# Cosine attention and an MLP mixer on one core: two-tile scores, ScalarE norms, a permuted w2, and the last residual by DMA transposes and VectorE adds

## The chip, the cores and the metric

The kernel runs on one core of one Trainium2 chip. The metric is device microseconds of one execution, measured over several executions. TensorE does the matmuls, VectorE and GpSimd elementwise work, ScalarE activations; SP issues most transfers, GpSimd those that cast.

In the profile's lines PE is TensorE, PEld its weight loads, DVE is VectorE, ACT is ScalarE, POOL is GpSimd, and SPq is SP issuing transfers. A matmul's recorded duration contains pipeline latency (a residual matmul is recorded with 219 ns, while the next one starts 56 ns later), so I measure a matmul's cost from one start to the next.

## The reference, cut to what matters

```python
q_n = q / (norm(q) + 1e-6);  k_n = k / (norm(k) + 1e-6)         # (8, 12, 448, 64)
attn = softmax(q_n @ k_n.T / tau)
x = (attn @ v) as (8, 448, 768)
h = relu(x.T @ w_tok1) @ w_tok2            # mixing over the 448 tokens
u = x + h.T
out = u + relu(u @ w_ch1) @ w_ch2          # (8, 448, 768), float32
```

## The kernel before

The unit of work is a pair of heads; there are 48 pairs, six per batch. Iteration i of the main loop computes the scores of pair i, attn @ v of pair i-1, and the token mixing of an earlier pair; once a batch's six pairs are done, its channel mixing (12 units `m_ch1`, then 6 or 8 output units `m_ch2`) is fed in between. For q and k the squares are made on GpSimd, summed on VectorE, and turned into 1/(norm + eps) by ScalarE and VectorE.

```python
ps = ctx.enter_context(tc.tile_pool(name="ps", bufs=4, space=PSUM))
ps2 = ctx.enter_context(tc.tile_pool(name="ps2", bufs=1, space=PSUM))
# ... cut ...
    def sums(i):
        lo = 2 * NCH * (i % HP)
        nc.vector.tensor_reduce(out=half[i // HP]["ssq"][:, :, lo:lo + 2 * NCH], in_=pipe[i]["sq"][:],
                                axis=AXX.X, op=ALU.add)

    def rnorms(n, p0=0, p1=HP):
        # ... cut ...
        nc.scalar.activation(out=rn, in_=ssq, func=AF.Ln, bias=tiny[:])
        nc.scalar.activation(out=rn, in_=rn, func=AF.Exp, scale=0.5)
        nc.vector.tensor_scalar_add(out=rn, in0=rn, scalar1=EPS_NORM)
        nc.vector.reciprocal(out=rn, in_=rn)

    def score(i, cg):
        # ... cut ...
        psS = ps2.tile([128, 2, 2, 512], FP32, name=f"psS_{i}_{cg}", tag="s")       # four banks, one buffer
        # four matmuls of 448 columns
        nc.scalar.activation(out=st["pt"][:, cg], in_=psS[0:SC, :, :, 0:S], func=AF.Exp, scale=inv_tau)

    def m_tok2(i):
        # ... cut ...
        for tt in range(TT):
            nc.tensor.matmul(psU[:], st["r"][:, tt, :], w2t[:, tt, 0:S], start=(tt == 0), stop=False)
        for c in range(NCH):                    # adds x; writes every fourth column of psU
            nc.tensor.matmul(psU[:].rearrange("d (p c) -> d c p", c=NCH)[:, c, :], st["x"][:, c, :],
                             id16[:, LEAD[c]:LEAD[c] + SC], start=False, stop=(c == NCH - 1))
        # VectorE copies psU to ut (u transposed, fp16)

    def m_ch2(b, m, dh):
        # ... cut ...
        for ct in range(CT):
            nc.tensor.matmul(psF[:], rows(gt, ct), wc2t[:, ct, dh * DH:(dh + 1) * DH],
                             start=(ct == 0), stop=False)
        for i in range(3):                      # the residual: u comes back through an identity
            nc.tensor.matmul(psF[:, 128 * i:128 * (i + 1)], rows(ut, 3 * dh + i), id16[:],
                             start=False, stop=(i == 2))
        if dh == 0:
            nc.vector.tensor_copy(out=o[:, 0:DH], in_=psF[:])
        else:
            nc.scalar.copy(out=o[:, DH:D], in_=psF[:])
    # ... cut ...
    # main loop, end of iteration i
            for p in sq_at.get(i, ()):
                sums(p)
                if p < 15:
                    rnorm1(p)                   # ScalarE: stands ahead of the exps of pair i+1
```

## Time and profile before

| | before |
|---|---|
| time, median of the first 3 runs | 456.56 us (456.43 to 456.67) |
| span of the profiled run | 455.0 us |
| TensorE busy, whole span / first 100 us | 408.4 us / 59.8 us |
| first score of iteration 8 / 10 / 13 | 66.6 / 95.0 / 118.1 us |
| from iteration 13 to the end | 336.9 us |

The last two rows are read from the timeline of TensorE: the start of the first score matmul of the iteration.

The page of the kernel before: busy tenths in 40 slices of the span, and the granted TensorE clock in tenths.

```profile
PE   1377572899999999999999999999999999999995
...
PEclk9999987899999999999999999999999999999998
```

There are two regimes. From the ninth slice on TensorE is at 9 all the way; before, it is not, and in the seventh slice the clock falls too. The table of busy time by stretch puts numbers on it (columns: stretch, its length, busy us of each engine with its instruction count, granted clock, mean busy share of the 16 DMA engines, which is over 1 where packets overlap in time, and GB/s):

```profile
20.00:40.00 20.00, 15.12 (x168) 10.04 (x168) 11.39 (x27) 12.44 (x13) 16.77 (x18) 1.00 1.14 243
40.00:60.00 20.00, 13.48 (x194) 9.98 (x191) 12.69 (x30) 11.22 (x12) 14.52 (x15) 0.92 0.84 174
60.00:80.00 20.00, 9.46 (x120) 6.04 (x117) 15.25 (x23) 7.20 (x11) 16.69 (x17) 0.84 0.75 147
...
120.00:160.00 40.00, 39.47 (x406) 23.90 (x404) 16.41 (x38) 23.08 (x27) 20.20 (x20) 1.00 0.51 132
```

Between 60 and 80 us no engine is full. That is the sign of a chain that runs from engine to engine. ScalarE's timeline of the kernel before shows its shape (start, duration, engine, line, operation, then idle time before it and what ended it):

```profile
62.10 0.31 ACT L162 ACTIVATE rn_382<-ssq_381,tiny 112x16 f32<-112x16 f32 x1 [2.58 <-DVE ssq_381 L155]
62.44 0.22 ACT L163 ACTIVATE rn_382<-rn_382 112x16 f32<-112x16 f32 x1
62.56 1.65 ACT L210 ACTIVATE pt_827<-psS_0_828 112x1792 f16<-112x1792 f32 x1
```

The exp at 62.56 us had its scores in PSUM since about 61 us, but stood behind the norms of a later pair (L162), and these waited 2.6 us for VectorE's sum. TensorE in turn waits for the exp. VectorE's timeline of the kernel before, around the largest loss:

```profile
69.20 0.17 DVE L164 TENSOR_SCALAR rn_382<-rn_382 112x16 f32<-112x16 f32 x1 [0.62 <-ACT rn_382 L163]
...
71.36 6.27 DVE L164 TENSOR_SCALAR rn_382<-rn_382 112x16 f32<-112x16 f32 x1 [0.62 <-ACT rn_382 L163]
```

The same add takes 0.17 us once and 6.27 us the next time. GpSimd's timeline over the second one has no gap:

```profile
71.57 1.05 POOL L176 TENSOR_TENSOR qn_924<-qh_378,rn_382 112x512 f16<-112x512 f32 x1
72.58 1.04 POOL L176 TENSOR_TENSOR kn_926<-kh_379,rn_382 112x512 f16<-112x512 f32 x1
73.58 1.03 POOL L150 TENSOR_TENSOR sq_928<-qh_701 112x512 f32<-112x512 f32 x1
...
76.57 1.03 POOL L150 TENSOR_TENSOR sq_931<-kh_702 112x512 f32<-112x512 f32 x1
77.55 0.88 POOL L112 DMA_DIRECT2D wc2t<-in_moe_w_ch_dram  x1
```

The add ends as soon as GpSimd turns to issuing a transfer (77.55 us). In the TensorE-bound part, two groups of matmuls are worth timing by their starts. TensorE's timeline of the kernel before, with the token mixing of one pair:

```profile
280.03 0.55 PE L254 MATMUL psU_4085<-w2t,r_4058 128*128 128x448 f16 x2
280.42 0.55 PE L257 MATMUL psU_4085<-id_83,x_3905 128*128 128x112 f16 x4
280.76 0.71 PE L221 MATMUL psO_1_4094<-vt_97,pt_3898 112*128 112x65 f16 x16
```

The four identity matmuls (L257) take 280.76 - 280.42 = 0.34 us, 85 ns each. And two output units at the end of the same timeline:

```profile
433.18 2.11 PE L288 MATMUL psF_0_0_6218<-wc2t,gt_3_4834 128*128 128x384 f16 x12
435.13 0.33 PE L291 MATMUL psF_0_0_6218<-id_83,ut_3_4833 128*128 128x128 f16 x3
435.30 2.11 PE L288 MATMUL psF_0_1_6235<-wc2t,gt_3_4834 128*128 128x384 f16 x12
```

The three residual matmuls (L291) take 435.30 - 435.13 = 0.17 us of the unit's 2.12. The twelve before them take 435.13 - 433.18 = 1.95 us, 162 ns for 384 columns each; by the same rate 112 columns would need 47 ns, an estimate that the prediction uses.

### The profile page before, as it was taken

To read this page: it belongs to the slowest core of one execution; us is meant where nothing else is said; L and a number is where in the kernel's file an instruction comes from. 1 tells how busy PE (TensorE), PEld (TensorE's weight loads), DVE (VectorE), ACT (ScalarE), POOL (GpSimd) and SP (SyncE) were. 2 spreads that over 40 slices of the span, in tenths; PEclk is the share of its full clock that TensorE was granted. 3 is DMA by queue.
4 is the path that set the end of the run, shared out by engine and by line. 5 is a ranking of instruction groups with operands and counts; after the bars stand their busy time and mean duration, and the time that the engine had idled before them with its cause. 6 is when DMAs were issued, how large, how long until landed. Compare 5 with 4: busy or idle time off the path is not lost.

```text
span 455.0 us, 9700 instructions
## 1 busy us (share of the span) xinstructions
PE 408.4 (90%) x4104; PEld 250.4 (55%) x4104; DVE 202.8 (45%) x458; ACT 236.8 (52%) x277; POOL 213.5 (47%) x216
## 2 busy tenths in 40 slices
PE   1377572899999999999999999999999999999995
PEld 0146451466655666556655666556656665566563
DVE  3656758565444354444534445446343433232000
ACT  3466543475466545675466455665565447630410
POOL 2686779391919265563838091926474330000000
PEclk9999987899999999999999999999999999999998
DMA  8999877752775169662685279733852233001012
GB/s 212 250 254 239 145 182 109 141 134 71 176 177 154 27 179 159 168 161 68 167 177 143 61 134 218 193 86 98 195 83 77 58 110 56 1 1 71 35 51 89
DMA packets 76411, 58.11 MB, mean 128 GB/s; under 512 B 36976, under 2 KB 72784, under 8 KB 76368
## 3 DMA queue, kind: packets, MB, share of 16 engines
q1 hardware_dynamic: 72704, 52.32, 48.0%
q0 software_dynamic: 3664, 5.18, 6.9%
q8 instruction: 32, 0.52, 0.5%
q14 instruction: 11, 0.09, 0.1%
HBM read 43.38 MB, written 11.01 MB: 120 GB/s over the span
## 4 chain that ended last, share of the span: by engine, by line
PE 80%; DVE 7%; ACT 6%; POOL 4%; issue 2%; DMA 1%; SPq 0%; ACTq 0%; POOLq 0%
DVE rn_382 L164 1%; DVE ssq_130 L155 1%; DVE ssq_381 L155 1%; DMA kh_104<-in_k_dram 1%; ACT pt_308 L210 1%; DVE ssq_118 L155 1%; DVE ssq_704 L155 0%; PE psG_2_1016 L269 0%; PE psF_1_0_3760 L288 0%; PE psF_1_0_2231 L288 0%; PE psF_0_0_2105 L288 0%; PE psF_2_1_1719 L288 0%; PE psF_1_0_5275 L288 0%; PE psF_1_1_1595 L288 0%; PE psF_0_1_1466 L288 0%
## 5 line engine op out<-in xcount | busy, mean ns | idle before, releaser
L269 PEld LDWEIGHTS <-wc1t 128*128 128x128 f16 x576 | 53.8, 101 | 45.1 <-issue 7.2
L233 PEld LDWEIGHTS <-w1t 128*128 128x128 f16 x384 | 22.7, 98 | 0.0
L288 PEld LDWEIGHTS <-gt_0_449 128*128 128x128 f16 x168 | 15.7, 98 | 10.9 <-issue 1.9
L288 PEld LDWEIGHTS <-gt_3_4834 128*128 128x128 f16 x168 | 15.9, 98 | 9.3
L288 PEld LDWEIGHTS <-gt_1_1784 128*128 128x128 f16 x168 | 15.8, 98 | 9.4 <-issue 0.4
L288 PEld LDWEIGHTS <-gt_2_3305 128*128 128x128 f16 x168 | 15.7, 98 | 9.5 <-issue 0.4
L188 PE MATMUL pst_156<-id_83,kn_154 112*128 112x112 f16 x4 | 0.6, 294 | 9.0 <-DVE kn_154 L176 9.0
L294 DVE COPY ost_0_6217<-psF_0_0_6218 128x384 f32<-128x384 f32 x1 | 0.6, 559 | 17.3 <-PE psF_0_0_6218 L291 17.3
L188 PE MATMUL pst_990<-id_83,kn_817 112*128 112x112 f16 x4 | 0.5, 286 | 8.1 <-DVE x_950 L225 8.1
L164 DVE TENSOR_SCALAR rn_382<-rn_382 112x16 f32<-112x16 f32 x3 | 6.6, 2206 | 1.9 <-ACT rn_382 L163 1.9
L176 POOL TENSOR_TENSOR qn_5263<-qh_4628,rn_4632 112x512 f16<-112x512 f32 x1 | 1.0, 1043 | 13.5 <-DVE rn_4632 L165 13.5
L176 POOL TENSOR_TENSOR qn_3745<-qh_3099,rn_3103 112x512 f16<-112x512 f32 x1 | 1.0, 1042 | 13.5 <-DVE rn_3103 L165 13.5
L176 POOL TENSOR_TENSOR qn_2216<-qh_1570,rn_1574 112x512 f16<-112x512 f32 x1 | 1.0, 1043 | 12.4 <-DVE rn_1574 L165 12.4
L176 POOL TENSOR_TENSOR qn_4510<-qh_3880,rn_3884 112x512 f16<-112x512 f32 x1 | 1.0, 1042 | 12.4 <-DVE rec_0_4542 L224 12.4
L176 POOL TENSOR_TENSOR qn_2981<-qh_2351,rn_2355 112x512 f16<-112x512 f32 x1 | 1.0, 1042 | 11.3 <-DVE rec_0_3013 L224 11.3
L176 POOL TENSOR_TENSOR qn_2611<-qh_1952,rn_1956 112x512 f16<-112x512 f32 x1 | 1.0, 1042 | 11.1 <-DVE rn_1956 L165 11.1
L176 POOL TENSOR_TENSOR qn_1839<-qh_1193,rn_1197 112x512 f16<-112x512 f32 x1 | 1.0, 1042 | 10.5 <-DVE rn_1197 L165 10.5
L176 POOL TENSOR_TENSOR qn_1452<-qh_808,rn_812 112x512 f16<-112x512 f32 x1 | 1.0, 1042 | 10.1 <-PE psO_0_1485 L221 10.1
L162 ACT ACTIVATE rn_107<-ssq_106,tiny 112x16 f32<-112x16 f32 x3 | 0.9, 307 | 9.1 <-DVE ssq_106 L155 9.1
L176 POOL TENSOR_TENSOR qn_4132<-qh_3481,rn_3485 112x512 f16<-112x512 f32 x1 | 1.0, 1044 | 9.6 <-DVE rn_3485 L165 9.6
L188 PEld LDWEIGHTS <-kn_154 112*128 112x128 f16 x4 | 0.3, 130 | 9.0 <-DVE kn_154 L176 9.0
L176 POOL TENSOR_TENSOR qn_4889<-qh_4246,rn_4250 112x512 f16<-112x512 f32 x1 | 1.0, 1042 | 9.0 <-DVE rn_4250 L165 9.0
(1681 smaller groups left out, 1266.8 us busy)
## 6 DMA issues: line engine op xcount, KB each, us to landing
wc1t<-in_moe_w_ch_dram POOLq DMA_DIRECT2D x2, 1152.0 KB, 10.9
wc2t<-in_moe_w_ch_dram POOLq DMA_DIRECT2D x2, 1152.0 KB, 9.5
qh_103<-in_q_dram SPq DMA_DIRECT2D x3, 224.0 KB, 4.3
kh_104<-in_k_dram SPq DMA_DIRECT2D x3, 224.0 KB, 4.6
vs_105<-in_v_dram SPq DMA_DIRECT2D x1, 672.0 KB, 7.0
qh_115<-in_q_dram SPq DMA_DIRECT2D x3, 224.0 KB, 8.1
kh_116<-in_k_dram SPq DMA_DIRECT2D x3, 224.0 KB, 8.3
vs_117<-in_v_dram SPq DMA_DIRECT2D x1, 672.0 KB, 10.7
```

What stands on the lines that cost most here:

```text
L155: nc.vector.tensor_reduce(out=half[i // HP]["ssq"][:, :, lo:lo + 2 * NCH], in_=pipe[i]["sq"][:], axis=AXX.X, op=ALU.add)
L162: nc.scalar.activation(out=rn, in_=ssq, func=AF.Ln, bias=tiny[:])
L164: nc.vector.tensor_scalar_add(out=rn, in0=rn, scalar1=EPS_NORM)
L176: eng.tensor_tensor(out=dst[:].rearrange("p c g e -> p g c e"), in0=src, in1=_bcast_free(rn, E), op=ALU.mult)
L188: nc.tensor.transpose(pst[:, a, c, :], src[:, c], id16[:SC, :SC])
L210: nc.scalar.activation(out=st["pt"][:, cg], in_=psS[0:SC, :, :, 0:S], func=AF.Exp, scale=inv_tau)
L233: nc.tensor.matmul(psR[:, tt, :], w1t[:, m, tt * 128:(tt + 1) * 128], st["x"][:, m, :], start=(m == 0), stop=(m == NCH - 1))
L269: nc.tensor.matmul(psG[:], wc1t[:, dt, ct * 128:(ct + 1) * 128], ut[:, dt, span(b)], start=(dt == 0), stop=(dt == DT - 1))
L288: nc.tensor.matmul(psF[:], rows(gt, ct), wc2t[:, ct, dh * DH:(dh + 1) * DH], start=(ct == 0), stop=False)
L294: nc.vector.tensor_copy(out=o[:, 0:DH], in_=psF[:])
```

## The change

There are three parts. I call them S, W and R.

- **S, schedule:** scores go to two 2-bank PSUM tiles instead of one of four banks; the norms stay on ScalarE to the end; squares, sums and norms move earlier, and norms come behind the exps of the current pair. Some transfers move too: the first half of the weight wc2 is loaded in iteration 6 instead of 7.
- **W, permuted w2:** the columns of w2 are reordered once, so that the identity matmuls that add x write PSUM densely. The copy of u to SBUF then puts the order back.
- **R, residual:** u is transposed back by DMA transposes on SP, and VectorE adds it while the output leaves PSUM. 168 identity matmuls go.

```diff
-    ps2 = ctx.enter_context(tc.tile_pool(name="ps2", bufs=1, space=bass.MemoryType.PSUM))
+    ps2 = ctx.enter_context(tc.tile_pool(name="ps2", bufs=2, space=bass.MemoryType.PSUM))
 ... rnorms
-        nc.vector.tensor_scalar_add(out=rn, in0=rn, scalar1=EPS_NORM)
-        nc.vector.reciprocal(out=rn, in_=rn)
+        nc.scalar.activation(out=rn, in_=rn, func=AF.Ln, bias=eps[:])
+        nc.scalar.activation(out=rn, in_=rn, func=AF.Exp, scale=-1.0)
 ... score, now for chunks c0 to c1
+        for c in range(c0, c1):
+            psS = ps2.tile([128, 2, 512], FP32, name=f"psS_{i}_{c}", tag="s")
+            # two matmuls, then the exp of this chunk alone (112x896)
 ... m_tok2
-        psU = ps.tile([128, S], FP32, name=f"psU_{i}", tag="b")
+        psU = ps.tile([128, NCH, SC], FP32, name=f"psU_{i}", tag="b")
+            nc.tensor.matmul(psU[:], st["r"][:, tt, :], w2t[:, tt], start=(tt == 0), stop=False)
+            nc.tensor.matmul(psU[:, c, :], st["x"][:, c, :], id16[:, LEAD[c]:LEAD[c] + SC],
+                             start=False, stop=(c == NCH - 1))
+        def rows(lo, n, p0, p1):
+            nc.vector.tensor_copy(out=ut[:, dt, lo:lo + n].rearrange("d (p c) -> d c p", c=NCH),
+                                  in_=psU[:, :, p0:p1])
+        # ... cut: rows() for the one or two ranges of u
+        nc.sync.dma_start_transpose(out=urt[b][:, dt, 0:n], in_=ut[:, dt, lo:lo + 128 * n])
 ... m_ch2
-        for i in range(3):
-            nc.tensor.matmul(psF[:, 128 * i:128 * (i + 1)], rows(ut, 3 * dh + i), id16[:], ...)
-        if dh == 0: ... VectorE copy   else: ... ScalarE copy
+        nc.vector.tensor_tensor(out=o[:, dh * DH:(dh + 1) * DH].rearrange("p (i d) -> p i d", i=3),
+                                in0=psF[:].rearrange("p (i d) -> p i d", i=3),
+                                in1=urt[b][:, 3 * dh:3 * dh + 3, j, :], op=ALU.add)
 ... schedule
-    sq_at = at({p: p - 3 if p < 10 else max(p - 6, 2 + p // 2) for p in range(3, NP_ALL)})
+    sq_at = at({p: p - 4 if p < 12 else max(p - 6, (p + 2) // 2) for p in range(4, NP_ALL)})
+    rn_at = at({p: p - 3 if p < 12 else (p + 4) // 2 for p in range(3, 15)})
-            for p in sc_at.get(i, ()):
-                scaled(p, dve="k" if p < 4 else "")
+            scaled(p, dve="k" if p < 7 else "")      # k on VectorE for three more pairs
 ... cut: the rest of the reordering
```

More of the change, by code (lines that the diff above doesn't have):

```diff
@@ L81 @@
     nc.gpsimd.memset(tiny[:], 1e-18)
+    eps = cst.tile([SC, 1], FP32, name="eps")
+    nc.gpsimd.memset(eps[:], EPS_NORM)
     w1t = cst.tile([128, NCH, T], FP16, name="w1t")
-    w2t = cst.tile([128, TT, S + 384], FP16, name="w2t")
+    w2n = cst.tile([128, TT, S], FP16, name="w2n")
+    w2t = cst.tile([128, TT, NCH, SC], FP16, name="w2t")
     wc1t = cst.tile([128, DT, C], FP16, name="wc1t")
@@ L98 @@
     pairt = {}
+    urt = {}
     def weights_tok():
@@ L103, in weights_tok, with place_w2 @@
         nc.gpsimd.dma_start(out=w1t[128 - SC:128, 3, :], in_=w1r[:, 3, :])
-        nc.gpsimd.dma_start(out=w2t[:, :, 0:S], in_=moe_w_tok2.rearrange("(tt p) s -> p tt s", p=128))
+        nc.gpsimd.dma_start(out=w2n[:], in_=moe_w_tok2.rearrange("(tt p) s -> p tt s", p=128))
+    def place_w2():
+        for tt in range(TT):
+            nc.gpsimd.tensor_copy(out=w2t[:, tt], in_=w2n[:, tt].rearrange("t (p c) -> t c p", c=NCH))
     def weights_ch1(i):
@@ L140, in sides, with squares @@
         return hf["q"][:, j:j + 2], hf["k"][:, j:j + 2]
-    def squares(i, on_act=False):
-        st = pipe[i] = {}
-        sq = nrm.tile([SC, 2, 2 * NCH, E], FP32, name=f"sq_{i}", tag="sq", bufs=2)
+    def squares(i, on_act=""):
+        if i not in pipe:
+            pipe[i] = {"sq": nrm.tile([SC, 2, 2 * NCH, E], FP32, name=f"sq_{i}", tag="sq", bufs=2)}
+        sq = pipe[i]["sq"]
         for a, src in enumerate(sides(i)):
             src = src.rearrange("p g c e -> p (g c) e")
-            if on_act:
+            if not on_act:
+                nc.gpsimd.tensor_mul(out=sq[:, a], in0=src, in1=src)
+            elif "qk"[a] in on_act:
                 nc.scalar.activation(out=sq[:, a], in_=src, func=AF.Square)
-            else:
-                nc.gpsimd.tensor_mul(out=sq[:, a], in0=src, in1=src)
-        st["sq"] = sq
     def sums(i):
@@ L188, in tpose, with qk_copy @@
                 nc.tensor.transpose(pst[:, a, c, :], src[:, c], id16[:SC, :SC])
-        nc.vector.tensor_copy(out=qk_tile(i)[:], in_=pst[:])
+        st["pst"] = pst
+    def qk_copy(i):
+        nc.vector.tensor_copy(out=qk_tile(i)[:], in_=pipe[i]["pst"][:])
     def dma_tpose(i):
@@ L195, in dma_tpose, with score @@
             nc.sync.dma_start_transpose(out=qk[:, a], in_=src[:].rearrange("p c g e -> p (c g e)"))
-    def score(i, cg):
+    def score(i, c0, c1):
         st = pipe[i]
         qk = st["qk"][:].rearrange("p a c s -> p (a c s)")
-        if cg == 0:
-            st["pt"] = ptp.tile([SC, 2, 2, 2, S], FP16, name=f"pt_{i}", tag="pt")
-        psS = ps2.tile([128, 2, 2, 512], FP32, name=f"psS_{i}_{cg}", tag="s")
-        for j in range(2):
-            c = 2 * cg + j
+        if c0 == 0:
+            st["pt"] = ptp.tile([SC, NCH, 2, S], FP16, name=f"pt_{i}", tag="pt")
+        for c in range(c0, c1):
+            psS = ps2.tile([128, 2, 512], FP32, name=f"psS_{i}_{c}", tag="s")
             for hh in range(2):
                 hb = hh * 64
-                nc.tensor.matmul(psS[:, hh, j, 0:S], qk[hb:hb + 64, c * SC:c * SC + 128],
+                nc.tensor.matmul(psS[:, hh, 0:S], qk[hb:hb + 64, c * SC:c * SC + 128],
                                  qk[hb:hb + 64, S:2 * S], start=True, stop=True)
-        nc.scalar.activation(out=st["pt"][:, cg], in_=psS[0:SC, :, :, 0:S], func=AF.Exp, scale=inv_tau)
+            nc.scalar.activation(out=st["pt"][:, c], in_=psS[0:SC, :, 0:S], func=AF.Exp, scale=inv_tau)
     def pv(i, hh):
@@ L220, in pv @@
             for c in range(NCH):
-                nc.tensor.matmul(psO[:, m, 0:E + 1], st["pt"][:, c // 2, hh, c % 2, lo:lo + 128],
+                nc.tensor.matmul(psO[:, m, 0:E + 1], st["pt"][:, c, hh, lo:lo + 128],
                                  vt[:, g, c, 0:E + 1], start=(c == 0), stop=(c == NCH - 1))
@@ L251, in m_tok2 @@
         ut = pairt[b // 2][0]
-        psU = ps.tile([128, S], FP32, name=f"psU_{i}", tag="b")
+        psU = ps.tile([128, NCH, SC], FP32, name=f"psU_{i}", tag="b")
         for tt in range(TT):
-            nc.tensor.matmul(psU[:], st["r"][:, tt, :], w2t[:, tt, 0:S],
-                             start=(tt == 0), stop=False)
+            nc.tensor.matmul(psU[:], st["r"][:, tt, :], w2t[:, tt], start=(tt == 0), stop=False)
         for c in range(NCH):
-            nc.tensor.matmul(psU[:].rearrange("d (p c) -> d c p", c=NCH)[:, c, :], st["x"][:, c, :],
-                             id16[:, LEAD[c]:LEAD[c] + SC], start=False, stop=(c == NCH - 1))
+            nc.tensor.matmul(psU[:, c, :], st["x"][:, c, :], id16[:, LEAD[c]:LEAD[c] + SC],
[3 more added lines that the diff above has]
+                                  in_=psU[:, :, p0:p1])
         if b % 2 == 0:
-            nc.vector.tensor_copy(out=ut[:, dt, 0:S], in_=psU[:])
+            rows(0, S, 0, SC)
         else:
-            nc.vector.tensor_copy(out=ut[:, dt, S + 64:2 * S], in_=psU[:, 0:384])
-            nc.vector.tensor_copy(out=ut[:, dt, S:S + 64], in_=psU[:, 384:S])
+            rows(S + 64, 384, 0, 96)
+            rows(S, 64, 96, SC)
+        n = 3 + b % 2
+        if b not in urt:
+            urt[b] = mix.tile([128, DT, 4, 128], FP16, name=f"ur16_{b}", tag="ur16")
+        lo = (b % 2) * 384
+        nc.sync.dma_start_transpose(out=urt[b][:, dt, 0:n], in_=ut[:, dt, lo:lo + 128 * n])
     def m_ch1(b, ct):
@@ L288, in m_ch2 @@
             nc.tensor.matmul(psF[:], rows(gt, ct), wc2t[:, ct, dh * DH:(dh + 1) * DH],
-                             start=(ct == 0), stop=False)
-        for i in range(3):
-            nc.tensor.matmul(psF[:, 128 * i:128 * (i + 1)], rows(ut, 3 * dh + i), id16[:],
-                             start=False, stop=(i == 2))
-        if dh == 0:
-            nc.vector.tensor_copy(out=o[:, 0:DH], in_=psF[:])
-        else:
-            nc.scalar.copy(out=o[:, DH:D], in_=psF[:])
+                             start=(ct == 0), stop=(ct == CT - 1))
+        j = m if b % 2 == 0 else (m + 1) % 4
+        nc.vector.tensor_tensor(out=o[:, dh * DH:(dh + 1) * DH].rearrange("p (i d) -> p i d", i=3),
+                                in0=psF[:].rearrange("p (i d) -> p i d", i=3),
+                                in1=urt[b][:, 3 * dh:3 * dh + 3, j, :], op=ALU.add)
+        if dh == NDH - 1:
             if m < 3:
@@ L308, in ch_units @@
         return ([(ns(S, DT), lambda ct=ct: m_ch1(b, ct)) for ct in range(CT)]
-                + [(ns(DH, 13), lambda m=m, dh=dh: m_ch2(b, m, dh))
+                + [(ns(DH, 12), lambda m=m, dh=dh: m_ch2(b, m, dh))
                    for m in range(3 + b % 2) for dh in range(NDH)])
@@ L330, in at, with gpsimd_part @@
         return got
-    load_at = at({p: p - 6 if p < 13 else max(p - 8, (p - 1) // 2) for p in range(9, NP_ALL)})
-    sq_at = at({p: p - 3 if p < 10 else max(p - 6, 2 + p // 2) for p in range(3, NP_ALL)})
+    load_at = at({p: p - 6 if p < 13 else max(p - 8, 6) for p in range(9, NP_ALL)})
+    sq_at = at({p: p - 4 if p < 12 else max(p - 6, (p + 2) // 2) for p in range(4, NP_ALL)})
+    rn_at = at({p: p - 3 if p < 12 else (p + 4) // 2 for p in range(3, 15)})
     sc_at = at({p: p - 2 if p < DMA_FROM else p - 3 for p in range(2, NP_ALL)})
     tok_at = at({p: max(p + 2, 3 if p < 1 else 4) for p in range(NP_ALL)})
+    EARLY = 8
+    def gpsimd_part(i):
+        for p in sc_at.get(i, ()):
+            scaled(p, dve="k" if p < 7 else "")
+        for p in sq_at.get(i, ()):
+            squares(p)
+        if i == 1:
+            weights_tok()
+        if i == 2:
+            place_w2()
+        if i in (2, 4):
+            weights_ch1(i // 4)
+        if i in (6, 8):
+            weights_ch2((i - 6) // 2)
+        if i and (i + 2) % HP == 0 and 1 <= (i + 2) // HP < NHALF:
+            cast_v((i + 2) // HP)
     with tc.manual_schedule():
-        load_qk(0)
-        load_qk(1)
+        for p in range(3):
+            load_qk(p)
         load_v(0)
-        for p in range(2, 5):
+        for p in range(3, 5):
             load_qk(p)
@@ L346 @@
             load_qk(p)
-        squares(0, on_act=True)
+        squares(0, on_act="qk")
         sums(0)
+        squares(1, on_act="q")
         rnorm1(0)
-        squares(1, on_act=True)
+        squares(1, on_act="k")
         squares(2)
@@ L353 @@
         tpose(0)
-        cast_v(0)
         sums(1)
+        qk_copy(0)
         rnorm1(1)
-        scaled(1, dve="qk")
+        scaled(1, dve="q")
         sums(2)
-        rnorm1(2)
+        squares(3)
         for i in range(NP_ALL + 2):
+            if DMA_FROM <= i + 2 < NP_ALL:
+                dma_tpose(i + 2)
             for p in load_at.get(i, ()):
@@ L364 @@
                 load_v((i + 4) // HP)
-            if DMA_FROM <= i + 2 < NP_ALL:
-                dma_tpose(i + 2)
-            for p in sc_at.get(i, ()):
-                scaled(p, dve="k" if p < 4 else "")
-            for p in sq_at.get(i, ()):
-                squares(p)
-            if i == 0:
-                weights_tok()
-            if i in (2, 4):
-                weights_ch1(i // 4)
-            if i in (7, 8):
-                weights_ch2(i - 7)
-            if (i + 2) % HP == 0 and 1 <= (i + 2) // HP < NHALF:
-                cast_v((i + 2) // HP)
+            if i:
+                gpsimd_part(i)
             left = 6 - (i - 2) % NPAIR
             quota = max(sum(t for t, _ in queue) - 2000.0, 0.0) / left
-            if i < NP_ALL:
-                score(i, 0)
+            if i < EARLY:
+                score(i, 0, 1)
+                score(i, 1, 2)
+            elif i < NP_ALL:
+                score(i, 0, 2)
+            if i == 0:
+                cast_v(0)
+                rnorm1(2)
+                gpsimd_part(0)
+                sums(3)
+            for p in rn_at.get(i, ()):
+                rnorm1(p)
             feed(quota * 0.25)
@@ L388 @@
                 m_tok1(p)
+            if i < EARLY:
+                score(i, 2, 3)
             feed(quota * 0.25, 400.0)
@@ L391 @@
                 tpose(i + 1)
-            if i < NP_ALL:
-                score(i, 1)
+                qk_copy(i + 1)
+            if i < EARLY:
+                score(i, 3, 4)
+            elif i < NP_ALL:
+                score(i, 2, 4)
             for p in tok_at.get(i, ()):
@@ L403 @@
                 sums(p)
-                if p < 15:
-                    rnorm1(p)
-                elif p % HP == HP - 1:
+                if p >= 15 and p % HP == HP - 1:
                     rnorms(p // HP)
```

## The prediction

> **What bounds the kernel now.** In the table of busy time by stretch, TensorE is busy 39.5 to 40.0 of every 40 us from 120 to 440 us: it is the bound there. In the first 100 us it is busy only 59.8 us, and its granted clock falls to 0.84. The timeline shows why. Each early exp stands on ScalarE behind a later pair's norms, which wait for a chain: GpSimd squares, VectorE sum (1.2 us), ScalarE Ln and Exp, VectorE add and reciprocal. So iterations 0 to 7 (first scores at 10.7 us, ninth pair's at 66.6 us) take 7.0 us each, though TensorE has some 3.6 us of work in each. At 71.4 us a VectorE add on 112x16 values takes 6.27 us (others 0.17) while GpSimd runs without a gap; TensorE idles 8.1 us. The Trainium skill ("SBUF — State Buffer", "Who interferes with whom") says that such an add can take the port pair shared with GpSimd, and that the loser blocks for the whole instruction; this trace agrees.
>
> **What changes, costed.**
>
> 1. Norms on ScalarE alone, squares one iteration earlier, norms after the scores in program order, scores in two 2-bank tiles instead of one of 4 banks. Per early iteration I estimate from traced durations: ScalarE 4.4 us (4 exps of 0.85, norms 0.9), VectorE 4.6, GpSimd 4.2, TensorE 3.6; with hand-overs 5.4 us. Iteration 8 would start near 54 us: -13 us. The 8.1 us stall, the slow clock behind it and smaller waits go: -10 us. A limit: loads ran at 250 GB/s early; by iteration 10 some 20 MB must have come, an estimated 72 to 80 us, where iteration 10 now starts at 95. So I take -20.
>
> 2. Residual matmuls: 168 of 128 columns, starting 53 ns apart in the timeline: -9 us, all TensorE-bound. (Their recorded 219 ns is latency.)
>
> 3. Permuted w2: the four 112-column identity matmuls that write PSUM with a step of four take 85 ns from start to start, where their columns need 47. Dense writes save 0.14 us a pair; for the 40 pairs in the TensorE-bound part -5.5 us.
>
> 4. Added: 48 DMA transposes (present ones take SP 1.2 us, land in 3.1 us; needed over 10 us later); 56 VectorE adds of about 0.56 us, 28 of them in place of copies; 96 more exp instructions (0.2 us each) less 28 copies on ScalarE. VectorE (45%) and ScalarE (52%) have room. Queueing on SP and VectorE: +1.5 us.
>
> **Sum.** -20 - 9 - 5.5 + 1.5 = -33, nearly all on the critical path: 456.6 becomes 423; I put 422 us, 412 to 434 for 8 in 10. Chances: faster by over 2% 0.97, within 2% 0.025, slower 0.005.
>
> **What would show it.** Right: iteration 8's first score before 58 us, no VectorE norm instruction but the sums, no TensorE wait over 4 us after 15 us, clock near 1; output units in the tail 1.95 us apart instead of 2.11; identity matmuls 47 to 55 ns apart; TensorE at 39.5 of 40 us from about 90 us on. Wrong: early iterations above 6 us; identity matmuls still 85 ns; TensorE waiting for adds or transposes.
>
> **What would make it wrong.** The early part bound by loads: wc2 late, TensorE waiting at the first output unit; loads standing behind transposes in SP's queue; VectorE's scaling of k (two inputs in SBUF) blocked by GpSimd as once before (1.60 us instead of 0.68). These give 430 or more. A smoother start gives 412.

## The result, and the profile after

Ratios here and below are the mean time of one kernel's fast runs over that of the other's of the same rounds, so not quite the ratio of the medians that I quote. A run over 1.5% above the fastest of its kernel counts as slow and is left out of the ratio: here the 435.32 us of the kernel after, below 444.88 us of s_only, three runs of spread, and one run (458.87 us) of the kernel before.

| | before | after |
|---|---|---|
| time, median of 4 | 456.5 us (456.25 to 456.67) | 431.34 us (428.05 to 435.32) |
| ratio, 95% interval | | 0.9425 (0.9372 to 0.9478) |
| span of the profiled run | 455.0 us | 428.9 us |
| iteration 8 / 10 / 13 starts | 66.6 / 95.0 / 118.1 us | 60.8 / 81.6 / 103.2 us |
| from iteration 13 to the end | 336.9 us | 325.7 us |

The gain is 25 us by the medians; 33 had been added up. The time lies inside the predicted range. In the profiled runs 14.9 us come before iteration 13 and 11.2 us after it. Note also the spread: the kernel before repeats within 0.4 us in this set, the kernel after within 7.

The page of the kernel after, the same lines as above:

```profile
PE   0467986999999999999999999999999999999995
...
PEclk9998698999999999999999999999999999999999
```

TensorE is at 9 to the end from the eighth slice (75 us) instead of the ninth (91 us), but the clock still has a hole, and the early slices are not full. The stretches of the kernel after (same columns):

```profile
20.00:40.00 20.00, 16.25 (x206) 10.28 (x203) 16.83 (x25) 15.16 (x28) 18.02 (x19) 0.91 0.85 163
40.00:60.00 20.00, 15.55 (x194) 10.26 (x195) 17.88 (x31) 13.78 (x29) 16.87 (x17) 0.83 1.16 227
60.00:80.00 20.00, 16.32 (x170) 9.66 (x168) 12.19 (x22) 14.61 (x31) 17.46 (x18) 0.91 1.15 232
...
120.00:160.00 40.00, 39.86 (x408) 23.48 (x408) 20.86 (x40) 23.50 (x38) 26.88 (x26) 1.00 0.68 171
```

Two things have changed there. VectorE is now nearly full from 20 to 60 us (17 of 20 us, where it had 11 to 13), and the DMA engines are full from 40 to 80 us. The first part of the loss is in the table of what TensorE waited for in the first 95 us of the kernel after (what waited, for what; total us, times, longest):

```profile
PE pst L196 <- DVE kn L184: 10.0, 1, 10.0
PE psS L218 <- ACT pt L220: 5.8, 5, 4.2
PE psU L264 <- DVE r L246: 4.1, 2, 3.8
PE psS L218 <- DVE qk L200: 4.0, 2, 3.3
PE pst L196 <- DVE x L235: 3.3, 1, 3.3
```

The first line is the start of the kernel, which was there before. The other four are waits of 4.2, 3.8, 3.3 and 3.3 us. The second and third of these lead to the same place. VectorE's timeline of the kernel after, before TensorE's wait that ends at 31.3 us:

```profile
26.49 3.71 DVE L184 TENSOR_TENSOR kn<-kh,rn 112x512 f16<-112x512 f32 x1
```

GpSimd's timeline of the same stretch:

```profile
26.16 1.48 POOL L143 CAST vt<-vs 112x1536 f16<-112x1536 f32 x1
27.59 1.05 POOL L184 TENSOR_TENSOR qn<-qh,rn 112x512 f16<-112x512 f32 x1
28.60 1.04 POOL L157 TENSOR_TENSOR sq<-qh 112x512 f32<-112x512 f32 x1
29.60 1.49 POOL L157 TENSOR_TENSOR sq<-kh 112x512 f32<-112x512 f32 x1
```

The scaling of k takes 3.71 us where its shortest takes 0.68, over GpSimd's work without a gap; when it gets through, GpSimd's own operation is stretched from 1.04 to 1.49. A second scaling of k, at 39.58 us, takes 3.06 us and leads to the wait of 3.8 us. So the add that lost 6.27 us is gone, but the change gave VectorE three more scalings of k (pairs 4 to 6) that can be kept waiting the same way.

The last wait, which ends at 68.6 us, has another chain. VectorE stood behind a sum, and the sum behind GpSimd's squares. GpSimd's timeline of the kernel after shows what these waited for:

```profile
60.03 1.04 POOL L157 TENSOR_TENSOR sq<-qh 112x512 f32<-112x512 f32 x1 [0.52 <-DMA qh<-in_q_dram]
...
63.29 1.04 POOL L157 TENSOR_TENSOR sq<-qh 112x512 f32<-112x512 f32 x1 [1.22 <-DVE ssq L163]
65.59 1.04 POOL L157 TENSOR_TENSOR sq<-kh 112x512 f32<-112x512 f32 x1 [1.26 <-DMA kh<-in_k_dram]
```

Loads account for 1.8 us of these waits, and VectorE's sum for 1.2.

The hole in the clock is three stretches at half clock: 32.6 to 36.0 us, 42.8 to 49.6 us and 70.1 to 73.5 us. They begin within 1.5 us of the ends of three of these waits, at 31.3, 43.6 and 68.6 us; the trace has none at the wait that ends at 19.6 us. The longest of them (same columns as above):

```profile
42.80:49.60 6.80, 6.02 (x58) 4.11 (x58) 6.00 (x11) 2.13 (x4) 5.17 (x5) 0.50 1.16 223
```

At half the clock the same two matmuls of the token mixing take 0.73 us (from 43.58 to 44.31 us), and 0.39 us later, at full clock (from 50.65 to 51.04 us). TensorE is busy for 12.8 us of the three stretches, so they cost it up to 6.4 us, an estimate from these figures. The kernel before has 13.7 us at half clock as well (56.7 to 60.1 and 73.7 to 84.0 us).

In the TensorE-bound part the work was removed as planned. TensorE's timeline of the kernel after, with the token mixing of a pair at full clock:

```profile
50.65 0.55 PE L264 MATMUL psU<-w2t,r 128*128 128x448 f16 x2
51.04 0.36 PE L266 MATMUL psU<-id,x 128*128 128x112 f16 x4
51.24 0.68 PE L231 MATMUL psO<-vt,pt 112*128 112x65 f16 x16
```

The identity matmuls take 0.20 us, 50 ns each, instead of 85. At the end of the same timeline the eight output units stand in one line:

```profile
408.44 15.76 PE L309 MATMUL psF<-wc2t,gt 128*128 128x384 f16 x96
```

15.76 us for eight (with the last one's latency); VectorE's adds behind them start 1.95 us apart, where the units took 2.12 before.

### The profile page after: what moved, and what is told of

It reads as the page before. It is cut to its first block, busy times and chain, and to the rows that moved or that the text cites. A ratio compares the mean times of both kernels' runs of the same rounds, so it can differ in the third digit from the quotient of the medians.

```text
span 428.9 us, 9560 instructions
## 1 busy us (share of the span) xinstructions
PE 392.4 (91%) x3936; PEld 230.0 (54%) x3936; DVE 228.8 (53%) x436; ACT 239.3 (56%) x397; POOL 214.4 (50%) x217
## 3 DMA queue, kind: packets, MB, share of 16 engines
q1 hardware_dynamic: 95744, 57.83, 59.3%
## 4 chain that ended last, share of the span: by engine, by line
PE 80%; DVE 9%; ACT 7%; issue 1%; POOL 1%; DMA 1%; SPq 0%; POOLq 0%; ACTq 0%
PE psG L290 25%; PE psF L309 24%; PE psO L231 10%; PE psS L218 9%; PE psU L264 5%; ACT pt L220 4%; PE psR L243 4%; DVE ssq L163 4%; PE psU L266 2%; DVE kn L184 2%; DMA qh<-in_q_dram 1%; POOL sq L157 1%; DVE x L235 1%; DVE ut L270 1%; ACT rn L172 1%
## 5 line engine op out<-in xcount | busy, mean ns | idle before, releaser
L220 ACT ACTIVATE pt<-psS 112x896 f16<-112x896 f32 x192 | 164.1, 914 | 61.1 <-PE psS L218 61.1
L290 PE MATMUL psG<-ut,wc1t 128*128 128x448 f16 x576 | 123.7, 355 | 0.0
L309 PE MATMUL psF<-wc2t,gt 128*128 128x384 f16 x672 | 117.2, 326 | 0.0
L292 ACT ACTIVATE gt<-psG 128x448 f16<-128x448 f32 x96 | 51.9, 546 | 73.0 <-PE psG L290 71.3
L270 DVE CAST ut<-psU 128x384 f16<-128x384 f32 (+1 forms) x72 | 55.8, 842 | 57.6 <-PE psU L266 57.5
L309 PEld LDWEIGHTS <-gt 128*128 128x128 f16 x672 | 63.0, 98 | 40.7 <-issue 3.2
L218 PE MATMUL psS<-qk 64*128 64x448 f16 x384 | 59.2, 370 | 14.0 <-ACT pt L220 9.5
L312 DVE TENSOR_TENSOR ost<-psF,ur 128x384 f32<-128x384 f32 x56 | 31.2, 558 | 73.4 <-PE psF L309 73.4
L231 PEld LDWEIGHTS <-pt 112*128 112x128 f16 x1536 | 61.2, 100 | 16.6 <-issue 7.4
L231 PE MATMUL psO<-vt,pt 112*128 112x65 f16 x1536 | 66.9, 196 | 0.0
L163 DVE TENSOR_REDUCE ssq<-sq 112x16 f32<-112x1024 f32 x48 | 58.0, 1210 | 10.9 <-POOL sq L157 5.6
## 6 DMA issues: line engine op xcount, KB each, us to landing
wc2t<-in_moe_w_ch_dram POOLq DMA_DIRECT2D x2, 1152.0 KB, 13.4
```

Source lines behind the costliest of these rows:

```text
L218: nc.tensor.matmul(psS[:, hh, 0:S], qk[hb:hb + 64, c * SC:c * SC + 128], qk[hb:hb + 64, S:2 * S], start=True, stop=True)
L220: nc.scalar.activation(out=st["pt"][:, c], in_=psS[0:SC, :, 0:S], func=AF.Exp, scale=inv_tau)
L231: nc.tensor.matmul(psO[:, m, 0:E + 1], st["pt"][:, c, hh, lo:lo + 128], vt[:, g, c, 0:E + 1], start=(c == 0), stop=(c == NCH - 1))
L270: nc.vector.tensor_copy(out=ut[:, dt, lo:lo + n].rearrange("d (p c) -> d c p", c=NCH), in_=psU[:, :, p0:p1])
L290: nc.tensor.matmul(psG[:], wc1t[:, dt, ct * 128:(ct + 1) * 128], ut[:, dt, span(b)], start=(dt == 0), stop=(dt == DT - 1))
L292: nc.scalar.activation(out=gt[:, ct, span(b)], in_=psG[:], func=AF.Relu)
```

## The experiments

Twelve kernels ran, in three sets of four, each set on a chip of its own and timed against the kernel before on that chip (spread, the last, some time after the other three of its set). The kernel before spreads more there than in the first comparison (451.9 to 458.9 us in one set). A single profiled run is therefore good for seeing which wait is there and how long it is, and less good for a difference of 2 or 3 us in the total; for that only the timed rounds count. All results were correct except the bench's.

### The three parts alone: r_only, w_only, s_only

r_only is the kernel before with R:

```diff
-        for i in range(3):
-            nc.tensor.matmul(psF[:, 128 * i:128 * (i + 1)], rows(ut, 3 * dh + i), id16[:], ...)
+        # transposes of ut in m_tok2, VectorE add here
```

> The kernel before with the residual part alone: 48 DMA transposes of u and VectorE adds instead of 168 identity matmuls. Theory (TensorE-bound part, 53 ns per matmul): 456.5 - 9 = 447.5 us, ratio 0.980; the early part up to iteration 10 unchanged at 95 us. Rival (transposes on SP and VectorE adds give some of it back): 451 us or more, with loads or TensorE waiting for them.

Measured: 450.57 us against 456.22, ratio 0.9882 (0.9805 to 0.996). Iteration 13 started at 119.1 us instead of 118.1, and from there to the end it took 329.8 us instead of 336.9. The time lies between the theory's 447.5 us and the rival's 451, nearer the rival; what the rival was made of is taken up below.

w_only is the kernel before with W:

```diff
-    w2t[:, :, 0:S] <- w2
+    w2n <- w2;  w2t[:, tt] <- w2n[:, tt] as "(p c) -> c p"   (GpSimd, once)
+    psU as [128, NCH, SC], identity matmuls dense, copy of u with a step of four on the write
```

> The kernel before with the permuted w2 alone. Theory: identity matmuls 50 ns from start to start instead of 85, 0.14 us a pair, -5 to -6 us: 450.5 to 451.5 us, ratio 0.988. Rival: the 1.17 us copies of u with a step of four (0.62 before) delay VectorE in the early part, where VectorE is on the chain, and give 2 us or more back: 453 us or more.

Measured: 449.78 us against 456.22, ratio 0.9888 (0.982 to 0.9955). Iteration 13 at 117.2 us, from there 330.4 us. The early part lost nothing, so the theory holds and the rival does not.

s_only is the kernel after with the parts of R and W taken back:

```diff
-    (after) VectorE adds, transposes of u, permuted w2
+    (before) identity residual, unpermuted w2, dense copy of u
```

> The kernel after with the identity residual and the unpermuted w2 put back, so the schedule, ScalarE norms and two-tile scores alone. Theory (the parts add up): 431 + 9 + 5.5 = 446 us, ratio 0.977. Rival (in the early part the step-of-four copies of u and the transposes cost several us that a kernel without them does not lose): 442 us or less, iteration 8 starting near 57 us instead of 60.8.

Measured: 440.52 us against 456.22, ratio 0.9653 (0.9574 to 0.9732). Iteration 8 started at 57.7 us, iteration 10 at 75.5, iteration 13 at 98.2, and from there it took 338.0 us.

Both signs of the rival came: the time is under 442 us and iteration 8 starts near 57; the theory's 446 us did not come.

What follows. By the ratios, taken of 456.2 us, S is worth 15.8 us, R 5.4, W 5.1: together 26.3, and the whole change 26.2 in its own comparison. So the measured parts add up within the intervals, and it is the predicted sizes of S and R that were too large. The profiled runs hint at more: s_only reached iteration 13 at 98.2 us, the kernel after only at 103.2. But its profiled run was the fastest of its four (438.2; the others 439.2, 441.9, 444.9), so a loss of some us by R and W in the early part is a reading of single traces, not of the timed rounds. The clock is part of that reading: s_only has one stretch at half clock, from 30.3 to 37.1 us, with TensorE busy for 4.7 us of it, where the kernel after has 12.8. By half of each that is 4 of the 5 us, an estimate; no run held the clock fixed, so this is not shown.

After iteration 13 the numbers are clean: R -7.1 us, W -6.5, S +1.1, sum -12.5; the kernel after has -11.2.

### The disputed costs by themselves: ports

A bench kernel. It runs VectorE scalings of 112x512 alone, then beside eight GpSimd squares; the same with the factors in PSUM; adds of 112x16; and copies of 128x448 out of PSUM. It writes zeros as output.

```diff
+    scale_sbuf(4); add(4)                       # alone
+    busy(8); scale_sbuf(4)                      # beside GpSimd
+    busy(8); scale_psum(4)                      # factors in PSUM
+    busy(8); add(4)
+    copies: dense; step of four on the write; step on the PSUM read
```

> A bench on its own, wrong result on purpose (zeros). VectorE scalings of 112x512 with two SBUF inputs, alone and while GpSimd runs eight squares back to back; the same with the factors in PSUM; adds on 112x16 in SBUF alone and beside GpSimd; copies of 128x448 from PSUM: dense, with a step of four on the write, with a step on the read. Port theory: scaling 0.68 us alone, 1.5 us or more for the first ones beside GpSimd, 0.68 with factors in PSUM; the adds 0.17 alone and over 1 us beside GpSimd. Rival (VectorE slowed by something else): no difference between beside and alone. Copies: 0.62 dense, 1.17 with the step on the write; a step on the read 0.62 if only writes suffer, 1.17 if both do.

Measured, from the bench's groups by line (count; minimum, median and maximum in ns): the scalings with factors in SBUF (L90, four alone and four beside GpSimd), those with factors in PSUM (L95, all beside GpSimd), and the adds (L100, four alone and four beside):

```profile
L90 DVE TENSOR_TENSOR dst<-src,rn x8: 682/691/1548, 5.1 to 12.8; 112x512 f16<-112x512 f32 x8
L95 DVE TENSOR_TENSOR dst<-src,pr x4: 678/686/686, 20.1 to 22.3; 112x512 f16<-112x512 f32 x4
L100 DVE TENSOR_SCALAR small<-small x8: 166/174/941, 7.9 to 31.2; 112x16 f32<-112x16 f32 x8
```

Beside GpSimd the four scalings took 5.15 us in all, where four alone took 2.86; with the factors in PSUM they took 2.84, beside the same GpSimd work. GpSimd's eight squares took 9.84 us beside the first kind and 8.86 beside the second. This is the port, and it is shown: one SBUF input instead of two, and the wait is gone on both sides. The Trainium skill ("SBUF — State Buffer", "Who interferes with whom") says so: a VectorE instruction with at most one SBUF input, outside the two-port modes, does not contend with GpSimd. The add, with one SBUF input, waited too (0.94 us instead of 0.17), so the number of inputs is not the whole condition. The longest wait in the bench, though, is under one GpSimd operation (a scaling of 1.55 us instead of 0.69). The waits of 3.7 and 6.3 us in the kernels, over three and more GpSimd operations, did not come up in the bench; why VectorE loses several times in a row there stays open.

The copies, in the order dense (L128), step on the write (L130), step on the read (L132):

```profile
L128 DVE CAST utile<-pv x4: 617/624/624, 41.4 to 43.3; 128x448 f16<-128x448 f32 x4
L130 DVE CAST utile<-pu x4: 1146/1146/1148, 44.0 to 47.5; 128x448 f16<-128x448 f32 x4
L132 DVE CAST utile<-pu x4: 624/624/625, 48.7 to 50.7; 128x448 f16<-128x448 f32 x4
```

So W costs VectorE 0.52 us a pair that its author need not pay: write densely and let the read of PSUM have the step.

### One wait at a time: rows_dense, ur_late, wc2_late, rn3_late

Four kernels, each the kernel after with one edit.

rows_dense:

```diff
-  out=ut[:, dt, lo:lo + n].rearrange("d (p c) -> d c p", c=NCH), in_=psU[:, :, p0:p1]
+  out=ut[:, dt, lo:lo + n].rearrange("d (p c) -> d p c", c=NCH), in_=psU[:, :, p0:p1].rearrange("d c p -> d p c")
```

> The kernel after, but the copy of u writes densely and reads PSUM with the step (0.62 us in the bench, where the step on the write took 1.15). Theory (the six early copies, 0.55 us each, lie on VectorE's chain while it is 17 of 20 us busy): iteration 10 starts 2 to 4 us earlier than 81.6, total 2 to 4 us less, ratio to the kernel before 0.937. Rival (VectorE has slack there too; the loss comes from the transposes or loads): iteration 10 within 1 us of 81.6 and the same time.

Measured: iteration 10 at 78.7 us instead of 81.6, iteration 13 at 101.1; but 430.97 us by the timed rounds, ratio 0.9449 (0.9392 to 0.9506). The early shift came as the theory had it, the total did not move beyond the intervals.

ur_late:

```diff
-  transposes of the first batch where u is made (iterations 3 to 7)
+  all six at the start of iteration 9, behind that iteration's loads
```

> The kernel after, but the six transposes of the first batch are issued together in iteration 9, behind that iteration's loads, so that no early load stands behind one. Theory (early loads delayed by transposes, which wait for VectorE in SP's queue): the load of pair 13 lands earlier, GpSimd's wait for it and TensorE's 3.3 us wait at 68.6 us shrink by 2 us or more, iteration 10 starts 2 to 3 us earlier. Rival (the DMA engines are simply full of weights and loads there): no change within 1 us.

Measured: TensorE's wait of 3.3 us became 2.0, iteration 10 at 80.0 us, iteration 13 at 101.7; 430.55 us, ratio 0.9456 (0.9397 to 0.9515). Between the theories: a shift of 1.6 us, and no gain in the total beyond the intervals.

wc2_late:

```diff
-        if i in (6, 8):
-            weights_ch2((i - 6) // 2)
+        if i in (8, 9):
+            weights_ch2(i - 8)
```

> The kernel after, but the two halves of wc2 are loaded in iterations 8 and 9 instead of 6 and 8. Theory (the loads of pairs 12 and 13 are slow, 9 us, because they share the DMA engines with the first half of wc2): GpSimd no longer waits for them, TensorE's 3.3 us wait at 68.6 us goes, iteration 9 starts 3 to 4 us earlier; total 2 to 4 us less if wc2 still comes in time, and TensorE waits at the first output unit (93.5 us) if not. Rival: no change within 1 us.

Measured: the wait of 3.3 us became 2.4, iteration 9 at 69.4 us instead of 73.4, iteration 10 at 77.6, iteration 13 at 99.2, and no wait for wc2; 429.0 us, ratio 0.9404 (0.9353 to 0.9456). The shift is the largest of the four; in the total it is 2 us of the medians, within the intervals. Of the 4 us, 1.5 were there at iteration 6 (50.4 us instead of 51.9), which is where the edit first acts: so much is scatter between single traces.

In ur_late and wc2_late GpSimd waited for no load of q or k between 46 and 88 us, so both edits did what they were for. What remained is its wait for VectorE (1.7 and 2.2 us, at 64.6 and 60.2 us), and TensorE's wait of 2.0 and 2.4 us behind it. Loads were only part of the 3.3 us.

rn3_late:

```diff
             for p in rn_at.get(i, ()):
-                rnorm1(p)
+                if i:
+                    rnorm1(p)
 ...
                 score(i, 3, 4)
+                if i == 0:
+                    rnorm1(3)
```

> The kernel after, but the norms of pair 3 come behind pair 0's last two exps on ScalarE. Theory (ScalarE stood 2.3 us with these exps behind norms that waited for VectorE, TensorE then waited 4.2 us): TensorE's wait at 19.6 us shrinks to about 1 us, iteration 1 starts near 16.5 us instead of 19.6; 1 to 3 us of it reach the end. Rival (VectorE and GpSimd set the pace from iteration 1 on): iteration 1 earlier, but iterations 3 and later start when they did, and no gain in the total.

Measured: iteration 1 started at 18.2 us instead of 19.6, iteration 3 at 31.4 as before, iteration 10 at 82.5; 432.43 us, ratio 0.9473 (0.9404 to 0.9541). The rival holds: the 4.2 us wait of iteration 0 (2.8 us here) was free, because iteration 3 waits for VectorE, behind the scaling of k, whatever comes before.

### The port wait removed: k_psum, three, three_k

k_psum is the kernel after, with the factors of k for pairs 2 to 6 handed over in PSUM:

```diff
+    def rn_psum(i):
+        pipe[i]["rk"] = ps.tile([SC, 2 * NCH], FP32, name=f"rk_{i}", tag="b")
+        nc.scalar.copy(out=pipe[i]["rk"][:], in_=half[i // HP]["rn"][:, 1, lo:lo + 2 * NCH])
+    def scaled_k(i):   # VectorE, in1 = rk in PSUM; placed behind m_tok1, one iteration earlier
```

> The kernel after, but for pairs 2 to 6 VectorE takes the factors of k from a small PSUM tile that ScalarE fills, so that the scaling has one SBUF input; one more ScalarE copy of about 0.2 us per pair, and the scaling of k moves up to the iteration of its norms. Theory (the 3.7 and 3.1 us scalings wait for the port that GpSimd holds; TensorE's waits of 3.3 us at 31 us and 3.8 us at 43.6 us come from them): every scaling of k on VectorE takes 0.7 us, both TensorE waits fall below 1 us, iteration 6 starts 5 us or more before 51.9; part of it, 2 to 5 us, reaches the end, loads permitting. Rival (VectorE is simply full there): scalings of 0.7 us but iteration 6 within 2 us of 51.9.

Measured: all five scalings took 0.69 us. Of the two TensorE waits, one became 0.5 us and the other 1.9, not below 1 as expected. Iteration 6 started at 46.0 us instead of 51.9, iteration 8 at 55.0 instead of 60.8: the theory's 5 us. The edit also moves the scaling of k one iteration earlier, and no run separates the two. And the kernel got slower: 438.44 us in four runs within 0.7 us, ratio 0.9595 (0.9569 to 0.9621). What TensorE waited for in its first 100 us:

```profile
PE pst L209 <- DVE x L248: 16.4, 1, 16.4
...
PE psS L231 <- DVE qk L213: 5.9, 3, 4.7
```

The 16.4 us are at 59 us, in iteration 8. VectorE stood behind a sum, the sum behind a square, and GpSimd's timeline of this kernel names the end of the chain:

```profile
50.39 0.88 POOL L120 DMA_DIRECT2D wc2t<-in_moe_w_ch_dram  x1
...
56.30 1.04 POOL L157 TENSOR_TENSOR sq<-kh 112x512 f32<-112x512 f32 x1
67.32 1.04 POOL L157 TENSOR_TENSOR sq<-qh 112x512 f32<-112x512 f32 x1 [9.97 <-DMA qh<-in_q_dram]
```

GpSimd waited 10 us for a load of q issued at 51.3 us, 0.9 us behind the first half of wc2 and right after a transpose of u that had held SP for 4.4 us; it landed at 67.2 us. The DMA engines were full (mean share 1.06 to 1.23 from 40 to 80 us). The iterations had become faster than the loads. three_k and spread, below, keep this edit and move the transfers; they run at 430.8 and 428.0 us, so the loss belongs to the transfers and not to the scaling.

three is the kernel after with the edits of rows_dense, ur_late and wc2_late together:

```diff
+ the three edits above
```

> The kernel after with dense copies of u, the first batch's transposes in iteration 9 and wc2 in iterations 8 and 9. Single runs moved the start of iteration 10 by 2.9, 1.6 and 4.0 us. Theory (three separate costs on one chain): together 5 to 8 us, iteration 10 near 75 us as in the kernel without the residual and w2 parts (75.5), total near 425 us. Rival (they remove the same wait): 77.6 us, as wc2 alone, and 429 us.

Measured: 433.15 us, ratio 0.948 (0.9433 to 0.9527); iteration 10 at 79.7 us, iteration 13 at 104.3. Neither number came: three gains that had each been seen alone did not add up.

three_k is three with k_psum's edit:

```diff
+ the three edits, and the factors of k in PSUM
```

> The three of the run before together with the factors of k in PSUM. Theory: the port's share (about 4 us by iteration 6) adds to the others: iteration 10 near 71 us, total near 421 us, close to the 422 that was predicted for the change. Rival: loads now set the pace (20 MB by iteration 10 at about 270 GB/s is 74 us), nothing more than the three alone, within 1 us.

Measured: 430.81 us, ratio 0.9422 (0.9371 to 0.9473). Iteration 8 at 57.4 us, iteration 10 at 75.1; then iteration 12 at 94.8 and 13 at 103.7, so the lead is gone (the kernel after: 96.1 and 103.2), and so are the theory's 421 us. TensorE waited 3.8 us for wc2 at the first output unit, and SP's own timeline shows another block:

```profile
68.55 19.20 SPq L298 DMA_TRANSPOSE ur<-ut  x7
87.86 1.67 SPq L220 DMA_TRANSPOSE qk<-kn  x1
```

Seven transposes of u in a row kept SP for 19.2 us, while half of the transposes of u in the kernel after hold SP for under 1.2 us each. The transposes of k and q for pair 12 stood behind them. Putting all six in one place only hurts once the iterations are faster.

### The transfers spread: spread

```diff
+    the factors of k in PSUM, dense copies of u
-    load_at = at({p: p - 6 if p < 13 else max(p - 8, 6) ...
+    load_at = at({p: {9: 2, 10: 2, 11: 3, 12: 4, 13: 4, 14: 5}.get(p, max(p - 8, 6)) ...
-        if i in (2, 4):
-            weights_ch1(i // 4)
+        if i in (1, 3):
+            weights_ch1(i // 2)
+    first batch's transposes: one per iteration, behind that iteration's loads
```

> The kernel after with the factors of k in PSUM and dense copies of u, and with the early transfers spread: q and k of pairs 9 to 14 loaded one to two iterations earlier, wc1 in iterations 1 and 3 (the DMA engines had gaps near 33 us), wc2 in 6 and 8 as in the kernel after, and the first batch's transposes one per iteration behind that iteration's loads. Theory (with the port wait gone the early part is bound by when loads and weights land; k_psum alone lost 16 us of TensorE to one load of pair 12, three_k lost 13 us to late wc2 and to seven transposes in a row): no TensorE wait above 3 us after 15 us, iteration 8 near 55, iteration 10 near 72 to 74, iteration 12 near 88, total 421 to 425 us. Rival (the DMA engines are full whatever the order, 20 MB and the transposes take until about 90 us): the waits move to the first output unit or to another load, and the total stays at 428 to 431 us.

Measured: six runs, 423.53, 425.85, 426.05, 429.89, 431.18 and 432.64 us; median 427.97 against 457.05; ratio 0.9304 (0.9268 to 0.9339). By the rule that a run over 1.5% above the fastest is slow, only the first three enter this ratio, and 429.89 us misses it by 0.01 us; all six would give 0.936. Their clocks (0.987 to 0.991) hardly differ from those of the other three (0.983 to 0.988), so I would not lean on the ratio alone. The profiled run was one of the slow ones (431.18 us). This is the fastest kernel by its median and by its fastest run. It beats the kernel before clearly. Against the kernel after, its interval lies below, but the two were timed in different sets, each against its own runs of the kernel before, and half its runs were set aside; a gain of about 1% is likely and not shown beyond doubt. Loads are not settled either: one run landed in the theory's 421 to 425 us and two within 1.1 us above it, one in the rival's 428 to 431 us and two above it.

### What the twelve have in common

In the profiled runs, the time from iteration 13 to the end depends only on R, W and S. (The twelve here are the kernels before and after and ten of the experiments: the bench has no iterations, and the profiled run of spread was a slow one.)

| kernel | iteration 8 | 10 | 13 | from 13 to the end |
|---|---|---|---|---|
| before | 66.6 | 95.0 | 118.1 | 336.9 |
| r_only | 66.2 | 96.5 | 119.1 | 329.8 |
| w_only | 67.4 | 94.5 | 117.2 | 330.4 |
| s_only | 57.7 | 75.5 | 98.2 | 338.0 |
| after | 60.8 | 81.6 | 103.2 | 325.7 |
| rows_dense | 59.9 | 78.7 | 101.1 | 325.2 |
| ur_late | 62.1 | 80.0 | 101.7 | 325.7 |
| wc2_late | 59.3 | 77.6 | 99.2 | 325.7 |
| rn3_late | 61.7 | 82.5 | 104.1 | 325.7 |
| k_psum | 55.0 | 88.7 | 110.3 | 325.7 |
| three | 62.2 | 79.7 | 104.3 | 325.2 |
| three_k | 57.4 | 75.1 | 103.7 | 325.3 |

All kernels with the whole change agree within 0.5 us after iteration 13. Every difference among them, and in these traces also their spread, is made before it, by the filling of the pipeline.

## Why the prediction was right or wrong

The direction, the range and the two regimes were right. The point value, 422 us, was 9 us too low: 25 us came instead of 33 to 34.

1. **"So I take -20" (the early part).** This is the first step that was mis-sized. S alone measured -15.8 us by the timed rounds; in the profiled run of the kernel after, iteration 10 came 13.4 us earlier and iteration 13 14.9 us earlier. The step under it, "with hand-overs 5.4 us" per early iteration, measured (60.8 - 11.7) / 8 = 6.1 us. The sums of busy time per engine that I took were about right, but they left out waits that no engine's own work contains: scalings of k of 3.7 and 3.1 us instead of 0.7, exps behind norms once more in iteration 0 (4.2 us, which rn3_late showed to cost nothing), and squares that waited for loads and for VectorE (3.3 us of TensorE). I also left out the step on the write of u (1.15 us instead of 0.62) in a stretch where VectorE is 17 of 20 us busy. The sign "iteration 8's first score before 58 us" failed (60.8), and so did "no TensorE wait over 4 us" (4.2) and "clock near 1" (0.83 from 40 to 60 us); "early iterations above 6 us", a sign of being wrong, came (6.1). "The slow clock behind it" was to go with the 8.1 us stall: the stall went, but 13.6 us at half clock remained, behind other waits. And the limit of "some 20 MB" by iteration 10 was too high: 17.9 MB had moved by then in the kernel before, 17.3 in the kernel after, and 17.1 in s_only, at 75.5 us.

2. **"168 x 53 ns: -9 us, all TensorE-bound."** The matmuls went and each output unit is 0.17 us shorter, as said. R alone gained 7.1 us after iteration 13, lost 1 us before it in its profiled run, and measured 5.4 us by the timed rounds, with an interval of 3.5 us to either side. The term was right as TensorE work and too large as time. Most of the rest is seen: 53 of the 56 output units come after iteration 13, which is 9.0 us, and after 100 us TensorE waited for exps 1.8 us in all in the kernel before, 3.3 in r_only and 3.7 in the kernel after. That leaves 7.5 us where 7.1 were measured.

3. **"-5.5 us" for the permuted w2.** Right: 50 ns instead of 85, W alone -5.1 us by the timed rounds and -6.5 after iteration 13. The Trainium skill ("PSUM — Partial Sum Buffer", "Specifications (TRN2)") says that any non-contiguous access pattern slows matmuls significantly; the trace agrees, with 85 against 50 ns for a step of four fp32 on the write.

4. **"Queueing on SP and VectorE: +1.5 us."** Too small where several resources are full at once, and it was counted as one lump for the whole run. After iteration 13 it is about 1.3 us (-11.2 against the -12.5 of the parts). Before it, single traces show up to 5 us (103.2 against s_only's 98.2); the timed rounds do not confirm that much, and by the estimate above most of it would be the clock.

5. **"What would make it wrong."** The two things named, the scaling of k kept waiting by GpSimd and loads that come late, are what the traces show (the 1.60 us quoted there was a scaling of q, at 13.1 us in the kernel before). Naming them in a list of risks and putting 1.5 us for them into the sum did not fit together.

What the experiments show of the early part is why it resists. Removing any one wait moved the next iterations by 1.4 to 4 us and left the total within the intervals, and removing the port wait made the kernel 7 us slower, because the iterations then ran into the transfers. By the first output unit (93.5 us in the kernel after) the kernel needs all of wc1 and wc2 (9.4 MB), w_tok1 and w_tok2 and q, k and v of some 14 pairs. In the kernel after, 20.1 MB had moved in the first 100 us; in the slices of 2.5 us in which the engines were full they moved 141 to 303 GB/s. What is left open: how much of the 6 us per early iteration each of the four resources would allow if the others were free, how much of it is the slow clock behind each wait, and why the times spread so much more than before.

## What to carry to other kernels

An estimate by the busy time per engine holds where one engine is full; where none is, add the waits, and when you remove one of them ask which transfer the faster engine will now run into. Cut the trace at the point from which all variants run alike (here iteration 13): the gains behind the cut are sums of instruction times (to 2 us here), the gains ahead of it are not. Count a TensorE wait together with the half clock that can follow it (3.4 to 6.8 us in the kernel after). A scaling moved to VectorE beside a busy GpSimd should take one of its two inputs from PSUM (the add with one SBUF input waited too), and a layout change that makes a matmul's write dense should leave its step on the PSUM read of the copy, not on its write.

## What the Trainium skill lacked or had wrong

- "SBUF — State Buffer", "Who interferes with whom": the loser of the shared port "fully blocks" until the winner's instruction ends. In the kernels VectorE lost several times in a row: 6.27 us for an add that takes 0.17, 3.71 us for a scaling that takes 0.68, over three and more GpSimd instructions. The page gives no bound for this. In the bench the wait was under one GpSimd instruction (a scaling of 1.55 us, an add of 0.94).
- The same page, note on cachelines (under "Door 1"): by it a step of 8 bytes on an fp16 access to SBUF should be free (two hits per line). For VectorE's copies of 128x448 from PSUM it was not: 1.15 us with the step on the write, 0.62 dense. The note says of PSUM that a non-contiguous pattern slows matmuls; it has nothing on VectorE's reads of PSUM, where a step of 112 fp32 cost nothing (0.62 us).
- "PSUM — Partial Sum Buffer", "Specifications (TRN2)": it says that a non-contiguous pattern slows matmuls, without a figure. Measured: 85 ns instead of 50 for 112 columns written with a step of four fp32.
- "DMA: Bandwidth & Descriptors" ("DMA Transpose (X-bar)"): no word on how long a transpose holds its issuer when many are in flight. One transpose of u held SP for 1.2 us (median) and at most 3.2 us in the kernel after, for up to 6.0 us in k_psum, and seven in a row for 19.2 us in three_k, with every later load and transpose of SP behind them.
